# Sorting tokens by expert while attention still runs: scatter per batch in place of one-hot inverses

## The chip, the cores and the metric

The kernel runs on one core of a Trainium2 chip. The metric is the device time of one execution in microseconds (us); three runs of the kernel before are given by their median. A profile of one further execution shows its engines: PE (TensorE matmuls), PEld (TensorE weight loads), DVE (VectorE), ACT (ScalarE), POOL (GpSimd), SP (SyncE, which here only issues DMAs).

## The reference

Two stages, eight batches of 576 tokens. First block-causal attention, eight heads of 64; a token of block i (64 tokens) sees blocks 0 to i:

```python
scores = scale * np.matmul(q, k.transpose(0, 1, 3, 2))       # q, k, v: (8, 8, 576, 64) f32
scores = np.where(block_i >= block_j, scores, -1000000000.0)
attn = softmax(scores); x = np.matmul(attn, v)               # x: (8, 576, 512)
```

Then each token goes to one of eight experts, and a token whose local gate is at least 0.5 takes the expert of the token before it:

```python
for b in range(B):
    prev_e = -1
    for s in range(S):
        fresh_e = int(np.argmax(logits[b, s]))                # logits = x @ w_gate
        e = fresh_e if s == 0 or local_gate[b, s] < 0.5 else prev_e
        prev_e = e
        p = softmax(logits[b, s])
        h = np.maximum(x[b, s] @ w1[e], 0.0)                  # w1: (8, 512, 1024)
        out[b, s] = p[e] * (h @ w2[e])                        # w2: (8, 1024, 512)
```

## The kernel before

**Attention** runs 32 iterations, one for a batch and two of its heads; four iterations make a batch. An iteration is a pipeline over several pairs: PE computes the scores of the next pair (L492, in three groups of banks), DVE their row maxima (`maxima`, L508), ACT the exponentials and their sums `rs` (`exps`, L516); PE transposes the probabilities of this pair (L526), DVE and ACT copy them to `pt`, PE multiplies by V (`attend`, L553), DVE copies the result to `ot` (L558). `inverse` (L562 to L567) adds the two sums of the last block and writes the reciprocals to `rv` with six DVE operations. `finish`, one iteration later, has PE turn `ot` and form the gate logits in the same matmul (L578); DVE multiplies by `rv`, the logits into `tmp` (L582) and the values into `xt` (L585); Pool adds the logits up (L590, L591); SP writes `xt` to `x_rows` in DRAM (L593, L594). Sixteen loads of expert weights, 1 MB each, are issued on Pool (L383) behind the gate adds of chosen iterations, from iteration 2 on. Instructions that are "pinned" keep the order of the program on their engine. `rs`, `nm` and `tmp` have two buffers each.

**Routing** has two calls: `routing(0)` for batches 0 to 5, its steps spread by `MIDDLE` and `BEHIND` over iterations 24 to 31, and `routing(1)` for batches 6 and 7, spread over the FFN's first tiles. It finds each token's own expert (L163 to L182), sends that through DRAM (`a_dram`, `row`) to have tokens along the free axis, carries the expert on by a scan (L202), returns through DRAM (`e_dram`, `ecr`), and ranks tokens within experts by matmuls with a triangle of ones. Each token so has a slot. The inverse, which token stands in a slot, comes from one-hots of the slot (`hot`, L336, L339, L343), matmuls of them (L350) and sums (L354, L356); its results are `tok_g` (row to gather), `tok_s` (row to scatter) and `pslot` (the probability).

**FFN** runs over 43 tiles of 128 slots, 20 of the first part, 23 of the second. All weights lie in SBUF. Per tile Pool gathers rows of `x_rows` (L665), PE transposes them (L674), DVE copies `xb` (L677) and the tile's first weights `wt` (`fetch`, L691); PE multiplies (`up`, L700), ACT applies relu (L707), but DVE the second half of it for tiles from 18 on (L709); PE multiplies by the second weights (L714), ACT scales by `pslot` (L719), and Pool scatters the rows to the output (L720). Outside attention the order on an engine is chosen by a scheduler when the program is built.

Of the kernel before, what the change touches and what calls it, by code (L numbers as in the profile page):

```python
# [16 lines left out]
def kernel(  # L17
# [11 lines left out]
    nc = tc.nc  # L29
# [38 lines left out]
    lg_all = w_p.tile([P, B * NJ, E + 1], F32, tag="lg_all", name="lg_all")  # L68

    x_dram = nc.dram_tensor("x_rows", [BS, Dm], BF16).ap()  # L70
# [4 lines left out]


    NB0 = 6
    NC0 = NB0 * NJ
    NT0 = -(-(NB0 * S - E * (P - 1)) // P)
    PARTS = [(0, NC0, NT0), (NC0, NC_, NT - NT0)]  # L80
    NTM = max(NT0, NT - NT0)

    OUT = 8192.0
# [12 lines left out]
    K = Const()  # L96

    def route_constants():
        K.id_b = rt([P, P], BF16, "id_b")
        nc.gpsimd.tensor_copy(K.id_b, id_f)  # L100
        K.iota_e = rt([P, E], F32, "iota_e")
        nc.gpsimd.iota(K.iota_e, pattern=[[1, E]], base=0, channel_multiplier=0,
                       allow_small_or_imprecise_dtypes=True)
        K.desc_e = rt([P, E], F32, "desc_e")
        nc.gpsimd.tensor_scalar(K.desc_e, K.iota_e, -1.0, float(E), op0=ALU.mult, op1=ALU.add)
        K.thr = rt([P, NTM], BF16, "thr")
        nc.gpsimd.iota(K.thr, pattern=[[1, NTM]], base=0, channel_multiplier=0,
                       allow_small_or_imprecise_dtypes=True)
        K.iota_lo = rt([P, P], BF16, "iota_lo")
        nc.gpsimd.iota(K.iota_lo, pattern=[[1, P]], base=0, channel_multiplier=0,  # L110
                       allow_small_or_imprecise_dtypes=True)
        K.ones_b = rt([P, P], BF16, "ones_b")
        nc.gpsimd.memset(K.ones_b, 1.0)

        tri_f = rt([P, P], F32, "tri_f", tag="big")
        nc.gpsimd.memset(tri_f, 1.0)
        nc.gpsimd.affine_select(out=tri_f, in_=tri_f, compare_op=ALU.is_gt, fill=0.0,
                                base=0, pattern=[[1, P]], channel_multiplier=-1)
        K.tri_b = rt([P, P], BF16, "tri_b")
        nc.gpsimd.tensor_copy(K.tri_b, tri_f)  # L120
        K.ones_e = rt([P, NC0 * E], BF16, "ones_e")
        nc.gpsimd.memset(K.ones_e, 1.0)

        K.val = rt([P, NC_, 5], BF16, "val")
        tmp = rt([P, NC_], F32, "chunk_id", tag="eqm")
        nc.gpsimd.iota(tmp, pattern=[[S // 64, B], [2, NJ]], base=0, channel_multiplier=0,
                       allow_small_or_imprecise_dtypes=True)
        nc.gpsimd.tensor_copy(K.val[:, :, 0], tmp)
        tmp = rt([P, 1], F32, "part1", tag="mx")
        nc.gpsimd.iota(tmp, pattern=[[0, 1]], base=1, channel_multiplier=1,  # L130
                       allow_small_or_imprecise_dtypes=True)
        nc.gpsimd.tensor_copy(K.val[:, :, 1], tmp.to_broadcast([P, NC_]))
        K.oh = rt([P, E, NC_], BF16, "oh")
        K.slot = rt([P, NC_], F32, "slot")
        K.off = rt([P, E], F32, "off")
        K.sub = rt([P, E], F32, "sub")
        K.taken = rt([P, E], F32, "taken")
        K.cnt = rt([P, E], F32, "cnt")

    pslots = [rt([P, x[2]], F32, "pslot%d" % k) for k, x in enumerate(PARTS)]  # L140
    tok_gs = [rt([P, x[2]], I32, "tok_g%d" % k) for k, x in enumerate(PARTS)]
    tok_ss = [rt([P, x[2]], I32, "tok_s%d" % k) for k, x in enumerate(PARTS)]
    te_is = [rt([1, x[2]], I32, "te_i%d" % k) for k, x in enumerate(PARTS)]

    def routing(k, ew, last, psum, pin):

        c0, c1, nt = PARTS[k]
        n = c1 - c0
        b0, b1 = c0 // NJ, c1 // NJ
        a_dram = nc.dram_tensor("a_dram%d" % k, [2, b1 - b0, NJ * P], BF16).ap()  # L150
        e_dram = nc.dram_tensor("e_dram%d" % k, [b1 - b0, NJ * P], BF16).ap()
        dve = nc.vector
        rows = [P, n, E]

        def ts(out, in_, a, b, op0=ALU.mult, op1=ALU.add):
            pin(dve.tensor_scalar(out, in_, a, b, op0=op0, op1=op1))

        def each(ap):
            return ap[:, :, None].to_broadcast([P, E, n])

        lg = lg_all[:, c0:c1, :E]
        mx = rt([P, n], F32, "mx")
        pin(dve.reduce_max(mx, lg, axis=AX))  # L163
        mx3 = mx[:, :, None].to_broadcast(rows)

        eqm = rt(rows, F32, "eqm")
        pin(dve.tensor_tensor(eqm, lg, mx3, op=ALU.is_ge))
        pin(ew.tensor_mul(eqm, eqm, K.desc_e[:, None, :].to_broadcast(rows)))
        ep = rt(rows, F32, "ep")
        pin(ew.tensor_sub(ep, lg, mx3))  # L170
# [3 lines left out]
        best = rt([P, n], F32, "best")  # L174
        pin(dve.reduce_max(best, eqm, axis=AX))
        ak = rt([P, 2, n], F32, "ak")
        pin(dve.tensor_single_scalar(ak[:, 1, :], lg_all[:, c0:c1, E], 0.0, op=ALU.is_ge))
        pin(dve.memset(ak[0:1, 1, 0:n:NJ], 0.0))
        ts(best, best, -1.0, float(E))
        nkeep = rt([P, n], F32, "nkeep")  # L180
        ts(nkeep, ak[:, 1, :], -1.0, 1.0)
        pin(dve.tensor_mul(ak[:, 0, :], best, nkeep))  # L182
# [5 lines left out]
        pin(nc.tensor.transpose(ps[:2 * n, :P], ak.rearrange("p a c -> p (a c)"), id_f))  # L188
        akT = rt([2 * n, P], BF16, "akT")
        pin(nc.scalar.copy(akT, ps[:2 * n, :P]))  # L190
        nc.sync.dma_start(out=a_dram.rearrange("a b (t p) -> (a b t) p", p=P), in_=akT)
        row = rt([b1 - b0, 2, S], BF16, "row", tag="ring", bufs=2)
        nc.sync.dma_start(out=row, in_=a_dram[:, :, :S].rearrange("a b s -> b a s"))
        sm = rt([P, n], F32, "sm")
# [5 lines left out]
        erow = rt([b1 - b0, NJ * P], BF16, "erow", tag="ring", bufs=2)  # L200
        pin(dve.memset(erow[:, S:], 0.0))
        pin(dve.tensor_tensor_scan(erow[:, :S], row[:, 1, :], row[:, 0, :], 0.0,  # L202
                                   op0=ALU.mult, op1=ALU.add))
        nc.sync.dma_start(out=e_dram, in_=erow)
        ecr = rt([n, P], BF16, "ecr", tag="akT")
        nc.sync.dma_start(out=ecr, in_=e_dram.rearrange("b (t p) -> (b t) p", p=P))
        yield

        ps = psum()
        pin(nc.tensor.matmul(ps[:, :n], lhsT=ecr, rhs=K.id_b[:n, :n], start=True, stop=True))  # L210
        eix = rt([P, n], F32, "eix", tag="best")
        pin(dve.tensor_copy(eix, ps[:, :n]))

        oh = K.oh[:, :, c0:c1]
        pin(dve.tensor_tensor(oh, eix[:, None, :].to_broadcast([P, E, n]),
                              K.iota_e[:, :, None].to_broadcast([P, E, n]), op=ALU.is_equal))
        pin(dve.memset(K.oh[64:, :, c0 + NJ - 1:c1:NJ], 0.0))

        pin(ew.tensor_mul(ep, ep, oh.rearrange("p e c -> p c e")))
# [4 lines left out]
        for x, m in enumerate((K.tri_b, K.ones_b)):  # L224
            pin(nc.tensor.matmul(ps[:, x * n * E:(x + 1) * n * E].rearrange(
                "p (e c) -> p e c", e=E), lhsT=m, rhs=oh, start=True, stop=True))
        rc = rt([P, 2, E, n], F32, "rc", tag="big")
        rc2 = rc.rearrange("p x e c -> p (x e c)")
        pin(nc.scalar.copy(rc2, ps[:, :2 * n * E]))
        pg = rt([P, n], F32, "pg")  # L230
        pin(dve.reduce_sum(pg, ep, axis=AX))
        pin(dve.tensor_mul(pg, pg, sm))
        pin(dve.tensor_copy(K.val[:, c0:c1, 2], pg))
        for j in (3, 4):
            pin(dve.tensor_sub(pg, pg, K.val[:, c0:c1, j - 1]))
            pin(dve.tensor_copy(K.val[:, c0:c1, j], pg))
        yield

        inc = rt([P, E, n], F32, "inc", tag="eqm")
        pin(dve.tensor_tensor_scan(inc.rearrange("p e c -> p (e c)"), K.ones_e[:, :n * E],  # L240
                                   rc[:, 1].rearrange("p e c -> p (e c)"), 0.0,
                                   op0=ALU.mult, op1=ALU.add))

        pin(dve.tensor_sub(inc, inc, rc[:, 1]))
        pin(dve.tensor_add(rc[:, 0], rc[:, 0], inc))
        cnt = rt([P, E], F32, "cnt_n")
        pin(dve.tensor_add(cnt, inc[:, :, n - 1], rc[:, 1, :, n - 1]))
        pin(dve.tensor_sub(cnt, cnt, inc[:, :, 0]))
        yield

        ci = rt([P, 2, E], I32, "ci")
        til = rt([P, E], F32, "til")
        end = rt([P, E], F32, "end")
        exc = rt([P, E], F32, "exc")
        base = rt([P, E], F32, "base")

        def tiles(c):
# [525 lines left out]
```

## Time and profile before

| | |
|---|---|
| median of three runs | 627.66 us (626.38 to 628.62) |
| the profiled execution | 625.85 us, its span 623.8 us |
| TensorE's mean granted clock | 0.975 |
| busy share of the span | PE 90%, DVE 73%, ACT 53%, Pool 25% |
| first score matmul (L492) | starts at 13.86 us |
| last `inverse` of attention (L562) | starts at 411.5 us |
| first up matmul of the FFN (L700) | starts at 429.81 us |
| scaled output of tile 0, of tile 42 (L719) | 436.4 us, 610.5 us |
| weight loads (L383) | 16, a median of 10.2 us from issue to landing |

The profile's page has the busy share of each engine in 40 slices, groups of instructions by line with their time, count, mean and the idle time ahead of them with what ended it ("<-DVE nm" means that a write of DVE to nm came last). Windows give busy time by stretch; the timeline lists instructions in order of their start with their duration.

### The profile page before, as it was taken

How to read it: one execution, taken by the hardware profiler on the slowest of the kernel's cores; microseconds unless marked ns; L12 is line 12 of the kernel's file. 1: busy time of each engine (PE TensorE's matmuls, PEld its weight loads, DVE VectorE, ACT ScalarE, POOL GpSimd, SP SyncE). 2: the span in 40 equal slices, each digit the busy share in tenths (PEclk: the TensorE clock that was granted, in tenths of full speed). 3: DMA queues.
4: the chain of work that ended last, by engine and by line, in shares of the span. 5: the costliest groups of instructions: out<-in, count | busy, mean ns of one | idle time of the engine just before them, and what ended most of it. 6: DMA issues, size and time to landing. Idle time of an engine off the chain costs nothing. (4 is left out here: it accounts for less than half of the span.)

```text
span 623.8 us, 15804 instructions
## 1 busy us (share of the span) xinstructions
PE 563.6 (90%) x5586; PEld 396.2 (64%) x5586; DVE 452.7 (73%) x1403; ACT 329.4 (53%) x1057; POOL 155.3 (25%) x218
## 2 busy tenths in 40 slices
PE   2899999999999999999999998765989899999991
PEld 1567667677677677666766665554667677766660
DVE  1688888888888888888888788894588855555540
ACT  1676676666666676666666765601444343323320
POOL 3000010010000001001010010144565565666532
PEclk9999999999999999999999999986999999999996
DMA  8246596595958668695874746102232222222210
GB/s 165 55 96 115 116 158 117 120 177 102 170 123 158 103 131 163 114 182 109 153 136 96 136 90 113 23 10 61 78 104 77 99 89 78 94 91 90 82 56 0
DMA packets 154078, 65.99 MB, mean 106 GB/s; under 512 B 138010, under 2 KB 146226, under 8 KB 154002
## 3 DMA queue, kind: packets, MB, share of 16 engines
q0 software_dynamic: 18048, 31.86, 24.8%
q1 hardware_dynamic: 132466, 32.52, 24.2%
q10 hardware_dynamic: 3488, 0.61, 0.6%
q8 instruction: 46, 0.75, 0.5%
q14 instruction: 30, 0.25, 0.1%
HBM read 67.55 MB, written 16.02 MB: 134 GB/s over the span
## 5 line engine op out<-in xcount | busy, mean ns | idle before, releaser
L516 ACT ACTIVATE pb<-ps_s,nm 128x512 f32<-128x512 f32 (+4 forms) x320 | 158.3, 501 | 97.8 <-DVE nm L508 97.3
L508 DVE TENSOR_REDUCE nm<-ps_s 128x1 f32<-128x512 f32 (+4 forms) x320 | 134.5, 453 | 54.0 <-ACT pb L516 31.8
L526 PE MATMUL ps_p<-id_f,pb 128*128 128x128 f32 (+1 forms) x800 | 105.1, 282 | 11.4 <-ACT pb L516 8.0
L492 PE MATMUL ps_s<-kT,qT 64*64 64x512 f32 (+7 forms) x1280 | 100.7, 419 | 6.1 <-ACT qT L475 6.1
L526 PEld LDWEIGHTS ps_p<-id_f,pb 128*128 128x128 f32 (+1 forms) x800 | 86.3, 141 | 24.7 <-ACT pb L516 10.0
L590 POOL TENSOR_TENSOR tmp<-tmp 128x45 f32<-128x45 f32 x32 | 8.5, 264 | 356.9 <-DVE tmp L582 356.9
L700 PEld LDWEIGHTS <-wt 128*128 128x128 bf16 x1376 | 81.1, 98 | 21.1 <-issue 15.8
L553 PE MATMUL ps_o<-pt,vt 128*64 128x320 f32 (+4 forms) x896 | 93.6, 360 | 0.0
L700 PE MATMUL ps_h<-xb,wt 128*128 128x128 bf16 x1376 | 84.3, 220 | 9.3 <-DVE xb L677 9.1
L714 PE MATMUL ps_o<-w_bf,hT 128*128 x344 | 86.6, 379 | 0.4
L553 PEld LDWEIGHTS ps_o<-pt,vt 128*64 128x64 f32 x896 | 59.3, 137 | 35.8 <-DVE tmp L582 4.9
L707 ACT ACTIVATE hT<-ps_h 128x512 bf16<-128x512 f32 x61 | 36.4, 597 | 79.1 <-PE ps_h L700 79.1
L720 POOL DMA_INDIRECT out_dram<-o_sb,tok_s x43 | 54.5, 1268 | 63.8 <-DMA out_dram<-o_sb,tok_s 21.0
L492 PEld LDWEIGHTS ps_s<-kT,qT 64*64 64x64 f32 x1280 | 45.4, 134 | 38.2 <-issue 23.6
L691 DVE COPY wt<-w_bf 128x4096 bf16 x43 | 53.1, 1238 | 15.5 <-PE ps_h L700 13.0
L516 ACT ACTIVATION_READ_ACCUMULATOR pb<-ps_s,nm 128x1 f32 x320 | 64.3, 201 | 0.0
L665 POOL DMA_INDIRECT xg<-x_rows,tok_g x43 | 55.3, 1286 | 22.6 <-PE ps_x L674 9.3
L719 ACT ACTIVATE o_sb<-ps_o,pslot 128x512 f32<-128x512 f32 x43 | 29.5, 687 | 44.0 <-PE ps_o L714 38.3
L709 DVE TENSOR_SCALAR hT<-ps_h 128x512 bf16<-128x512 f32 x25 | 17.3, 691 | 48.1 <-PE ps_h L700 48.1
L578 PE MATMUL ps_n<-wg,ot 128*128 128x146 f32 x320 | 49.4, 303 | 0.0
L541 ACT COPY pt<-ps_p 64x128 f32<-64x128 f32 (+2 forms) x102 | 43.6, 441 | 10.5 <-PE ps_p L526 10.3
L714 PEld LDWEIGHTS <-hT 128*128 128x128 bf16 x344 | 31.2, 98 | 24.8 <-issue 1.1
(147 smaller groups left out, 568.7 us busy)
## 6 DMA issues: line engine op xcount, KB each, us to landing
w_bf<-in_moe_w_dram POOLq DMA_DIRECT2D x16, 1024.0 KB, 10.2
natq<-in_q_dram SPq DMA_DIRECT2D x64, 128.0 KB, 2.6
vt<-in_v_dram SPq DMA_DIRECT2D x64, 128.0 KB, 4.7
natk<-in_k_dram SPq DMA_DIRECT2D x60, 128.0 KB, 2.7
x_rows<-xt SPq DMA_DIRECT2D x32, 128.0 KB, 2.6
natq<-in_q_dram SPq DMA_DIRECT2D x32, 32.0 KB, 2.5
vt<-in_v_dram SPq DMA_DIRECT2D x32, 32.0 KB, 6.3
natk<-in_k_dram SPq DMA_DIRECT2D x30, 32.0 KB, 2.2
```

The lines of the kernel that those rows point to most:

```text
L492: pin(nc.tensor.matmul(ps[y][f * 64:(f + 1) * 64, c:c + n], lhsT=qT[r, i * 64:(i + 1) * 64], rhs=kT[r, a:a + n], start=True, stop=True))
L508: pin(nc.vector.reduce_max(nm[:, z:z + 1], ps[g][y][:, c:c + n], axis=AX, negate=True))
L516: pin(nc.scalar.activation(pb[i][:, a:a + n], ps[g][y][:, c:c + n], func=AF.Exp, bias=nm[:, i:i + 1], accum_out=rs[:, z:z + 1]))
L526: pin(nc.tensor.transpose(ps[:kk, (c + e) * P:(c + e + 1) * P], pb[i0 + 2 * e][:, j * P:j * P + kk], id128))
L541: pin(cp(dst, src))
L553: pin(nc.tensor.matmul(ps[h * D:(h + 1) * D, a - q0:qn], lhsT=vts[i % 3][:, j, h, :], rhs=pt[j][:, h, a - j * P:a - j * P + n], start=(j = ...
L578: pin(nc.tensor.matmul(ps[:, (t - t0) * (P + WG):(t - t0 + 1) * (P + WG)], lhsT=ot[:, t * P:(t + 1) * P], rhs=wg[:, hp], start=True, stop= ...
L665: nc.gpsimd.indirect_dma_start(out=xg[:], out_offset=None, in_=x_dram[:rows], in_offset=bass.IndirectOffsetOnAxis(ap=tok_gs[k][:, u:u + 1] ...
L691: nc.vector.tensor_copy(wt.rearrange("p k f -> p (k f)"), w1_bf[:, bass.ds(o, WE)])
L700: nc.tensor.matmul(ps_h[:, f, :], lhsT=wt[:, ko, fo * P:(fo + 1) * P], rhs=xb[:, ko * P:(ko + 1) * P], start=(ko == 0), stop=(ko == KO1 - 1))
L714: nc.tensor.matmul(ps_o, lhsT=hT[:, fo, :], rhs=w2_bf[:, bass.ds(woff + fo * Dm, Dm)], start=(fo == 0), stop=(fo == FO - 1))
L720: nc.gpsimd.indirect_dma_start(out=out_flat, out_offset=bass.IndirectOffsetOnAxis(ap=tok_ss[k][:, u:u + 1], axis=0), in_=o_sb[:], in_offse ...
```

## The change

The rows of x are no longer written to DRAM in token order and gathered through an inverse. `finish` writes them to a tile of the batch, `x_b`, whose rows carry two more words: the token's number and its probability. As soon as a batch is complete, `routing(b)` works on that batch alone, by the same steps, with a running count `K.free` of the next free row of each expert's region in `x_sorted`; then five indirect DMAs scatter its rows to those regions, each through a view of its own, so that no scatter waits for another. The steps are hooked to iterations, nine places for each batch. `table(k)` computes from the counts which rows a tile gathers and which expert it has; the one-hots, `tok_g`, `tok_s` and `pslot` are gone. Tiles now read the token's number and probability from the gathered rows.

With it come: `inverse` takes one reciprocal on DVE and six copies on Pool; two buffers of V in place of three, with its loads later; k of the second pair and the gate weights are loaded from SP, and an Exp of one column is put ahead of the first copies; the first part has 16 tiles instead of 20, so DVE takes relus from tile 14 on; the 16 gathers of the first part are issued early, three in iteration 30 and the others behind the last gate add; output scatters go through views of their own as well; the tiles from 36 on add a skip to the token's number (`tok_e`).

```diff
-    x_dram = nc.dram_tensor("x_rows", [BS, Dm], BF16).ap()
+    ROW = Dm // 2 + 2
+    xs = nc.dram_tensor("x_sorted", [E * BS, ROW], I32).ap()
+    xs_views = dram_disjoint_views(xs, B * NJ)
+    out_views = dram_disjoint_views(out_flat, NT)
     NB0 = 6
-    PARTS = [(0, NC0, NT0), (NC0, NC_, NT - NT0)]
+    PARTS = [NB0 * S // P - E - 3, 0]
+    PARTS[1] = NT - PARTS[0]
...
+    def routing(b, x, lg, psum, pin, ew):
+        ...
+        pin(dve.tensor_add(rk[:, :NJ], rk[:, :NJ], K.free[:, None, :].to_broadcast(full)))
+        pin(dve.tensor_mul(rk[:, :NJ], rk[:, :NJ], oh))
+        to = rt([P, NJ], F32, "to")
+        pin(dve.reduce_sum(to, rk[:, :NJ], axis=AX))
+        to_i = rt([P, NJ], I32, "to_i", bufs=2)
+        pin(dve.tensor_copy(to_i, to))
+        pin(dve.memset(to_i[64:, NJ - 1:], E * BS))
+        pin(dve.tensor_add(K.free, K.free, rk[:, NJ]))
+        yield
+        for c in range(NJ):
+            pin(pool.indirect_dma_start(
+                out=xs_views[b * NJ + c], out_offset=bass.IndirectOffsetOnAxis(ap=to_i[:, c:c + 1], axis=0),
+                in_=x[:, c, :], in_offset=None, bounds_check=E * BS - 1, oob_is_err=False))
+            if c == 2:
+                yield
+        yield
...
-        vts = [cst.tile([P, NJ, 2, D], F32, tag="v%d" % x, name="vt") for x in range(3)]
+        vts = [cst.tile([P, NJ, 2, D], F32, tag="v%d" % x, name="vt") for x in range(2)]
...
-                eng = nc.scalar if nm == "k" and i < 2 else nc.sync
+                eng = nc.scalar if nm == "k" and i == 0 else nc.sync
...
+        warm = rt([P, 1], F32, "warm")
+        nc.vector.memset(warm, 0.0)
+        pin(nc.scalar.activation(warm, warm, func=AF.Exp))
...
-            nc.scalar.dma_start(out=wg[r, :, c:c + E], in_=gsrc[h])
-            nc.scalar.dma_start(out=wg[r, :, c + E:c + E + 1], in_=lsrc[h])
+            nc.sync.dma_start(out=wg[r, :, c:c + E], in_=gsrc[h])
+            nc.sync.dma_start(out=wg[r, :, c + E:c + E + 1], in_=lsrc[h])
...
         def inverse(rs):
             pin(nc.vector.tensor_add(rs[:, NB - 1:NB], rs[:, NB - 1:NB], rs[:, NB:NB + 1]))
+            pin(nc.vector.reciprocal(rs[:, :NB], rs[:, :NB]))
             for f in range(2):
                 r = slice(f * 64, (f + 1) * 64)
-                pin(nc.vector.reciprocal(rv[:64, 0:1, f ^ swap[0]], rs[r, 0:1]))
-                pin(nc.vector.reciprocal(rv[:64, 1:, f ^ swap[2]], rs[r, 2:NB:2]))
-                pin(nc.vector.reciprocal(rv[64:, :NJ - 1, f ^ swap[1]], rs[r, 1:NB:2]))
+                pin(nc.gpsimd.tensor_copy(rv[:64, 0:1, f ^ swap[0]], rs[r, 0:1]))
+                pin(nc.gpsimd.tensor_copy(rv[:64, 1:, f ^ swap[2]], rs[r, 2:NB:2]))
+                pin(nc.gpsimd.tensor_copy(rv[64:, :NJ - 1, f ^ swap[1]], rs[r, 1:NB:2]))
...
+        def hook(i, half):
+            if half == 1 and i % HP == 0 and i > 0:
+                b = i // HP - 1
+                steps[b] = routing(b, *batches[b], psum, pin, pool)
+                plan(steps[b], [(i, 1), (i + 1, 0), (i + 1, 1), (i + 2, 0), (i + 3, 0),
+                                (i + 3, 1), (i + 4, 0), (i + 4, 1), (i + 5, 0)])
+                if b == NB0 - 1:
+                    plan(table(0, pin), [(i + 4, 1), (i + 5, 0), (i + 5, 1)])
+            for x in reversed(todo.get((i, half), ())):
+                next(x, None)
+            if (i, half) == (HP * NB0 + HP + 2, 1):
+                gather_early()
...
-            if n == 0 or t < NT0 - 2:
+            if n == 0 or t < N0 - 2:
                 nc.scalar.activation(dst, ps_h, func=AF.Relu)
...
+            tok = xgs[t][:, Dm // 2:Dm // 2 + 1]
+            if t >= NCT:
+                tok_e = f_p.tile([P, 1], I32, tag="tok_e", name="tok_e")
+                nc.vector.tensor_tensor(tok_e, tok, skip_i[:, t - NCT:t - NCT + 1], op=ALU.add)
+                tok = tok_e
...
-                out=out_flat,
-                out_offset=bass.IndirectOffsetOnAxis(ap=tok_ss[k][:, u:u + 1], axis=0),
+                out=out_views[t],
+                out_offset=bass.IndirectOffsetOnAxis(ap=tok, axis=0),
...
+        with tc.issue_after(gate_last.ins):
+            while len(xgs) < N0:
+                gather_next()
```

## The prediction

> **What bounds the kernel now.** I read the page's slices first: they show the stages, and each has its own limit.
>
> ```profile
> PE   2899999999999999999999998765989899999991
> DVE  1688888888888888888888788894588855555540
> ACT  1676676666666676666666765601444343323320
> POOL 3000010010000001001010010144565565666532
> ```
>
> One slice is 15.6 us. Attention fills slices 2 to 26 with PE at nine tenths and DVE at eight; a hole follows; then the FFN, where Pool and DVE are half busy. The hole, by stretches (columns: PE, PEld, DVE, ACT, POOL busy us, clock, DMA share, GB/s):
>
> ```profile
> 400.00:410.00 10.00, 6.80 (x63) 5.62 (x65) 8.78 (x33) 4.41 (x17) 4.50 (x13) 1.00 0.06 15
> 410.00:420.00 10.00, 5.32 (x44) 4.45 (x40) 9.13 (x39) 0.00 (x0) 4.20 (x10) 0.75 0.01 3
> 420.00:430.00 10.00, 1.47 (x12) 0.94 (x11) 4.93 (x18) 0.27 (x1) 5.72 (x6) 0.50 0.20 51
> ```
>
> DVE is full there with the one-hots of the inverse (L336 to L356), PE is not. Next one steady iteration, in the timeline of all engines, since the change rewrites its end:
>
> ```profile
> 174.74 0.27 POOL L591 TENSOR_TENSOR lg_all<-lg_all,tmp 128x45 f32<-128x45 f32 x1
> ...
> 177.34 3.19 PE L526 MATMUL ps_p<-id_f,pb 128*128 128x128 f32 x25
> 177.39 0.31 ACT L516 ACTIVATE pb<-ps_s,nm 128x64 f32<-128x64 f32 x1 [0.29 <-DVE nm L508]
> ...
> 178.00 0.15 DVE L562 TENSOR_TENSOR rs<-rs 128x1 f32<-128x1 f32 x1
> 178.07 0.15 DVE L565 RECIPROCAL rv<-rs 64x1 f32<-64x1 f32 x1
> ...
> 182.37 0.69 ACT L516 ACTIVATE pb<-ps_s,nm 128x512 f32<-128x512 f32 x1 [1.54 <-DVE nm L508]
> ```
>
> I count everything from L562: it starts exactly every 11.9 us from 35.2 to 320.8, one per iteration, and from there to 403.1 the six iterations with routing take 82.3 instead of 71.4. The next iteration's first exp stands 4.4 us after L562. Last, the FFN and its end, Pool's queue in time:
>
> ```profile
> L720 POOL DMA_INDIRECT out_dram<-o_sb,tok_s x43 | 54.5, 1268 | 63.8 <-DMA out_dram<-o_sb,tok_s 21.0
> ...
> 613.60 0.98 POOL L720 DMA_INDIRECT out_dram<-o_sb,tok_s  x1 [1.87 <-issue]
> 616.45 0.98 POOL L720 DMA_INDIRECT out_dram<-o_sb,tok_s  x1 [1.87 <-DMA out_dram<-o_sb,tok_s]
> ```
>
> The last scatters stand 2.85 us apart, each behind the landing of the one before (2.8 us in the list of DMA issues), and 616.45 is five us after the last o_sb (610.5 + 0.69).
>
> **The change, part by part.** All against the profiled execution: span 623.8, time 625.85, which is 1.8 below the median 627.66.
>
> *Start.* ACT's table load starts at 11.81 because ACT's queue first issues eight k loads and wg; it takes 1.28, qT's copy 0.71, and scores start at 13.86 after 6.09 us of PE idle for qT. kT is done at 8.30. With a table load ahead and wg on SP, scores can start when kT is there, 8.5: **-5.3**. SP's queue gets seven more issues of 0.5 us, behind the loads of pair 0; if they hold pair 1 or wg back, some of it is lost: -3 to -5.5.
>
> *Routing per batch, in attention.* Per batch some 20 DVE operations of 128x40 or less (the trace's 128x80 ones take 0.24, its 128x10 ones 0.17) and a scan (1.35, L202): about 4.7 us of DVE, 3.7 of it ahead of group-2 maxima. Price: in the trace the first two steps (0.40 + 0.41 behind L562, 1.3 ahead of the maxima) made the iteration from 320.8 take 13.11, that is +1.2 for 2.1 us of DVE. At that rate 2.7 per batch; but most pieces are below the 0.7 us for which exps end ahead of the transposes, and the inverse gives DVE back 0.75 in every iteration (six reciprocals of 0.15 to 0.17 become one, the copies go to Pool). I take 1.3 per batch, seven batches: **+9**; between 0 (all in DVE's idle sixth) and +19. In iterations without a step I count the 0.75 as nothing, since PE covers it; if it is not, 0.3 x 31 = 9 comes back. x_rows' 64 writes leave SP, 28 small DMAs come; SP is no bound.
>
> *Scatters and the new wait.* Behind step six four scatters of a batch are queued on Pool, and behind them the six copies rv<-rs. In the built order the fourth copy waits for the landing of all four scatters. rs has two buffers, so the next iteration's first exp on ACT waits for the copies: it stands 4.4 us after L562. Queued behind Pool's wait are the fifth scatter and the gate adds; behind ACT's exp, PE's transposes; DVE's multiplies (finish) wait for rv too. In iterations 12 and 16 the scatters start some 2.9 us ahead of L562, 1.31 apart (1.01 plus 0.30, as the gathers stand), so the last lands at -2.9 + 3.9 + 2.8 = +3.8, three to six copies of about 0.25 (L590 as the nearest row) end at 4.6 to 5.3: **+1** for both. In iterations 8, 20, 24 and 28 a weight load stands directly ahead of them on the same software queue. The trace has no indirect DMA behind a weight load, so two bounds. Landing as if alone: 1 us later than above, 0.4 past slack each, +1.6 in all. Landing behind the load's own bytes (10.2 us median; 8.5 and 11.7 the extremes): -2.9 + 10.2 + 0.7 = +8.0 (0.7 for their rows: the out scatters' median landing of 2.8 above their minimum of 2.1), copies +8.75, ACT 4.4 late, less the 0.7 of slack: 3.7 each, 2 to 5.2 by the extremes. I take the second, since q0 software_dynamic is one row of the page for loads and scatters alike and three scatters behind each other have no other ring: **+15**, range +1.6 to +21.
>
> The Trainium skill, DMA: Bandwidth & Descriptors (Queues, rings and completion order), says that on each DMA engine descriptors of one ring are consumed in ring order, and its section SWDGE vs HWDGE vs iDMA that only one software queue is allocated. The trace cannot show it here. By that rule the term is the +15, and the design's intent, scatters hidden behind attention, is broken in those four iterations; without it, +1.6.
>
> *table(0)* about 25 DVE operations of 0.17 to 0.8 in iterations 28 and 29, 5 us at the rate above: **+3** (0 to 5). *One-hot inverse gone:* 82.3 - 71.4: **-10.9**. Attention in sum 9 + 1 + 15 + 3 - 10.9 = +17.1.
>
> *The hole.* From the last L562 (411.5) to the first up matmul (429.81) 18.3 us: DVE's one-hots to 419.4, finish, then fetch, gather, transposes. After: the first tiles are gathered, and behind finish (1.5 us) DVE has two wt copies of 1.23 and xb 0.42; about 6 us: **-12.3** (-9 to -13).
>
> *FFN.* Relus of the second half go to DVE from tile 14 instead of 18 and DVE's order is wt, xb, relu throughout: the loop of the trace's tiles 28 to 42, where relu 0.69, wt 1.22, xb 0.42 and PE's 1.95 follow each other, 4.27. Tiles 14 to 27 took 50.0 for 13, 3.85: +5.5. tok_e for the spare tiles stands in DVE's queue near tile 22 and waits for a gather that, with 17 buffers, waits for the out of tile 19: +3. Batch 7's scan is followed directly by the one-hot that waits for its round trip through e_dram; between scan and matmul the trace shows 3.2 us, then partly covered by a wt copy of 1.23: +2. Routing of batches 6 and 7 with table(1), 12 us of small operations beside DVE's wt and xb, takes the place of the trace's (tiles 0 to 14 took 60.6 at 3.85 x 14 = 53.9): 0. In sum **+10.5**; from +2 (no loop, no spike) to +24 (below).
>
> *Tail.* Scatters go to views of their own, so the last is issued when its o_sb is there, 611.5 instead of 616.45: **-5**; 0 if Pool is late by itself.
>
> Sum: -5.3 + 17.1 - 12.3 + 10.5 - 5 = +5.0. 625.85 + 5.0 = 630.9, and 1.8 for the median: 632.7.
>
> **Rivals.** *No wait behind the weight loads* (the other side): the term is +1.6 instead of +15, the sum -8.4, 619.3. It decides at one place: if the four scatters of iterations 8, 20, 24 and 28 land by +4.4 after L562, ACT waits for nothing. For it speaks that a load and a scatter touch different memory and 16 engines share the work; against it the single queue. Between 610 (with 0.3 per iteration back) and 625.
>
> *Pool bounds the FFN:* 13 gathers, ten scatters, then per tile an out and a gather that waits for an earlier out's landing. Out and gather together 1.27 + 1.29 + 2 x 0.30 = 3.2 fit; but in 500 to 547 single outs averaged 1.45, and 1.02 + 0.30 + landing 2.8 in a row would be 4.2 plus 0.3 to 0.5: 4.6 a tile in tiles 4 to 42 instead of 4.2: +14 over my sum, 647. For it: Pool's 0.5 to 0.6 already; against: 8.1 us of its idle time there is for ACT, so it has room.
>
> *Small operations hide, and the reciprocals' 0.75 shows:* 0 instead of +9 and -3 from the steady iterations: 621 to 625 with the scatter waits. For it DVE's 84%; against it PE's full slices.
>
> **How the numbers follow.** Chances: forecast 0.45 (626 to 645), no wait 0.30, Pool 0.13, hidden operations 0.12. 0.3% of 627.7, about what a measurement can tell from no change, is 1.9 us. Faster (below 625.8): 0.27 of the no-wait case, 0.08 of the hidden, 0.03 of the forecast, together 0.38; same 0.06; slower 0.56. The range reaches into the no-wait and Pool cases: 612 to 650.
>
> **What would show it.** Right: ACT's first exp of iterations 9, 21, 25 and 29 idle for 3 to 5 us with Pool's rv copy as the releaser, and those intervals of the inverse (then L539) near 16 us; scores at 8.5; up matmul 6 us after the last inverse; tiles at 4.27 from 14 on; last out issue within 1.5 us of its o_sb. Wrong: those intervals at 12 to 13 (no wait), o_sb periods above 4.5 with Pool never idle (Pool), routing iterations at 11.9 (hidden). The forecast falls most simply if a scatter behind a weight load lands in 3 us.

## The result, and the profile after

The changed kernel takes 676.67 us (675.29 to 677.38, four runs) beside 627.02 (622.03 to 628.62): 1.080 of the time before, interval 1.074 to 1.087. The direction was right, the size was not: +50 where +5 stood. The profiled execution has a span of 675.3 at a granted clock of 0.951; before it was 623.8 at 0.975. All stages below compare these two.

The page's slices of after; one slice is 16.9 us:

```profile
PE   5999999879999999969969996877996762688986
DVE  3687788858878778758866885863742440345552
ACT  4666666456656656636636653513442221123322
POOL 2002122312322331422141342376884444442222
```

Two things are new. Attention has notches (ACT at 4, 3, 3, 3, PE at 7 or 6), and in the FFN PE falls to 6, 7, 6, 2, 6 just after Pool stood at 7, 6, 8, 8. This is one of the notches in the timeline of Pool, around iteration 20, whose weight load is L354:

```profile
282.46 0.80 POOL L354 DMA_DIRECT2D w_bf<-in_moe_w_dram  x1
283.56 1.07 POOL L265 DMA_INDIRECT x_sorted<-x_b,to_i  x1 [0.30 <-DVE nm L483]
...
287.55 0.98 POOL L265 DMA_INDIRECT x_sorted<-x_b,to_i  x1 [0.30 <-issue]
288.52 0.21 POOL L543 COPY rv<-rs 64x1 f32<-64x1 f32 x1
...
295.52 0.18 POOL L543 COPY rv<-rs 64x1 f32<-64x1 f32 x1 [6.45 <-DMA x_sorted<-x_b,to_i]
```

Three copies run at once, the fourth waits 6.45 us for the landing of four scatters that stand behind a load. On ACT, in its timeline, the next exp waits with it:

```profile
296.09 0.69 ACT L491 ACTIVATE pb<-ps_s,nm 128x512 f32<-128x512 f32 x1 [7.04 <-POOL rv L545]
```

The list of ACT's waits (total us, times, longest) has all six such exps together:

```profile
ACT pb L491 <- POOL rv L545: 31.1, 6, 7.4
```

The list of line L265, the scatters, says who waited for them (us, times) and how long they took to land:

```profile
  POOL rv L543: 28.0, 6
...
DMA to landing us min/median/max: 2.3/3.0/9.8
```

The hole is smaller. Windows of after, with the columns of the prediction's; last inverse (L539) at 441.52, first up matmul at 447.26:

```profile
430.00:440.00 10.00, 8.31 (x72) 6.30 (x70) 7.49 (x25) 4.29 (x17) 3.14 (x13) 1.00 0.00 1
440.00:450.00 10.00, 5.82 (x62) 5.27 (x59) 7.05 (x31) 1.03 (x3) 6.78 (x15) 0.79 0.08 20
450.00:460.00 10.00, 9.89 (x100) 7.68 (x101) 4.62 (x5) 4.50 (x8) 8.17 (x7) 0.87 0.31 88
```

In the FFN, DVE's timeline shows one long wait, and Pool's an even rhythm behind it:

```profile
555.72 0.42 DVE L662 COPY xb<-ps_x 128x512 bf16<-128x512 bf16 x1
578.33 0.16 DVE L705 CUSTOM_DVE_ANT_0 tok_e<-xg,skip_i 128x2 uint16<-128x2 uint16 x1 [22.19 <-DMA xg<-x_sorted,rows]
578.41 0.69 DVE L694 TENSOR_SCALAR hT<-ps_h 128x512 bf16<-128x512 f32 x1
```

```profile
565.78 1.02 POOL L146 DMA_INDIRECT xg<-x_sorted,rows  x1 [2.50 <-issue]
567.10 1.02 POOL L709 DMA_INDIRECT out_dram<-o_sb,xg  x1 [0.31 <-issue]
570.62 1.02 POOL L146 DMA_INDIRECT xg<-x_sorted,rows  x1 [2.50 <-issue]
```

A pair of gather and out takes 4.84 here: 1.02, a gap of 0.30, 1.02, and 2.50 until the out just issued has landed (this one at 569.89). Other pairs take up to 6.5; from the gather of tile 24 to that of tile 42 the mean is 5.2. The out at 567.10 is tile 18's, and reads the token numbers from its `xg`; the gather at 570.62 is tile 35's, and with 17 buffers overwrites that one. Pool's order lets each gather run ahead as far as the buffers allow, so each waits for the out directly ahead of it. The tail:

```profile
670.09 0.98 POOL L709 DMA_INDIRECT out_dram<-o_sb,tok_e  x1 [3.22 <-ACT o_sb L708]
671.82 0.98 POOL L709 DMA_INDIRECT out_dram<-o_sb,tok_e  x1 [0.74 <-ACT o_sb L708]
```

The outs wait for their o_sb now, not for each other. By stages, profiled against profiled:

| stage | predicted | measured |
|---|---|---|
| start, to the first inverse (35.2, now 31.0) | -5.3 | -4.2 |
| attention, first to last inverse (376.3, now 410.5) | +17.1 | +34.2 |
| hole, to the first up matmul (18.3, now 5.75) | -12.3 | -12.5 |
| FFN, to the last o_sb (180.7, now 223.6) | +10.5 | +42.9 |
| tail, to the end (13.3, now 4.5) | -5 | -8.8 |
| sum | +5.0 | +51.6 |

### The profile page after: what moved, and what is told of

It reads as the page before. It is cut to its first block, busy times and chain, and to the rows that moved or that the text cites. A ratio compares the mean times of both kernels' runs of the same rounds, so it can differ in the third digit from the quotient of the medians.

```text
span 675.3 us, 15911 instructions
## 1 busy us (share of the span) xinstructions
PE 575.7 (85%) x5519; PEld 407.0 (60%) x5548; DVE 428.3 (63%) x1276; ACT 323.3 (48%) x1054; POOL 229.2 (34%) x488
## 5 line engine op out<-in xcount | busy, mean ns | idle before, releaser
L699 PE MATMUL ps_o<-w_bf,hT 128*128 x315 | 84.0, 386 | 33.6 <-DVE hT L694 16.6
L685 PEld LDWEIGHTS <-wt 128*128 128x128 bf16 x1376 | 88.3, 104 | 29.1 <-issue 23.2
L685 PE MATMUL ps_h<-xb,wt 128*128 128x128 bf16 x1376 | 91.9, 230 | 15.4 <-DVE xb L662 11.1
L467 PE MATMUL ps_s<-kT,qT 64*64 64x512 f32 (+7 forms) x1280 | 103.8, 430 | 0.7 <-DVE kT L453 0.7
L558 PE MATMUL ps_n<-wg,ot 128*128 128x146 f32 x320 | 53.0, 317 | 19.4 <-ACT qT L450 19.0
L146 POOL DMA_INDIRECT xg<-x_sorted,rows x40 | 49.2, 1231 | 55.7 <-issue 23.8
L708 ACT ACTIVATE o_sb<-ps_o,xg 128x512 f32<-128x512 f32 x40 | 27.5, 688 | 74.4 <-DMA out_dram<-o_sb,xg 47.5
L558 PEld LDWEIGHTS ps_n<-wg,ot 128*128 128x128 f32 x320 | 45.4, 205 | 22.6 <-ACT qT L450 19.9
L694 DVE TENSOR_SCALAR hT<-ps_h 128x512 bf16<-128x512 f32 x29 | 20.1, 692 | 60.5 <-PE ps_h L685 60.4
L543 POOL COPY rv<-rs 64x1 f32<-64x1 f32 x64 | 11.8, 185 | 134.3 <-DVE rs L540 59.2
```

Of the source, the lines that this page charges most:

```text
L146: nc.gpsimd.indirect_dma_start(out=xg[:], out_offset=None, in_=xs, in_offset=bass.IndirectOffsetOnAxis(ap=rows[k][:, u:u + 1], axis=0), bo ...
L467: pin(nc.tensor.matmul(ps[y][f * 64:(f + 1) * 64, c:c + n], lhsT=qT[r, i * 64:(i + 1) * 64], rhs=kT[r, a:a + n], start=True, stop=True))
L558: pin(nc.tensor.matmul(ps[:, (t - t0) * (P + WG):(t - t0 + 1) * (P + WG)], lhsT=ot[:, t * P:(t + 1) * P], rhs=wg[:, hp], start=True, stop= ...
L685: nc.tensor.matmul(ps_h[:, f, :], lhsT=wt[:, ko, fo * P:(fo + 1) * P], rhs=xb[:, ko * P:(ko + 1) * P], start=(ko == 0), stop=(ko == KO1 - 1))
L699: nc.tensor.matmul(ps_o, lhsT=hT[:, fo, :], rhs=w2_bf[:, bass.ds(woff + fo * Dm, Dm)], start=(fo == 0), stop=(fo == FO - 1))
L708: nc.scalar.activation(o_sb, ps_o, func=AF.Copy, scale=xgs[t].bitcast(F32)[:, Dm // 2 + 1:])
```

## The experiments

Each is timed against the kernel before on the same chip; line numbers shift by a few with an edit.

**The reciprocals back on DVE.** Theory: Pool's copies carry the wait into attention, and it is worth 15. Rival: DVE's work is the cost.

```diff
-            pin(nc.vector.reciprocal(rs[:, :NB], rs[:, :NB]))
...
-                pin(nc.gpsimd.tensor_copy(rv[:64, 0:1, f ^ swap[0]], rs[r, 0:1]))
+                pin(nc.vector.reciprocal(rv[:64, 0:1, f ^ swap[0]], rs[r, 0:1]))
```

(and so for all six.) 

> Undoes one part: the six reciprocals are back on DVE, so no copy on Pool stands behind the scatters. Theory (Pool's copies wait for the landing of scatters that stand behind a weight load, and ACT's next exp waits for the copies): the four intervals of 18.1 to 19.8 us between inverses fall to 12.5 to 13.5, iterations without routing go from 11.65 back to 11.9, in sum -23 + 31 x 0.25 = -15, about 661 us. Rival (the scatters' traffic or the weight load itself slows the iteration): these intervals stay above 17 and the time goes up by 8, to 684.

668.86, 1.069 (1.067 to 1.071): a gain of 7.8, half of what was expected. The four intervals fall from between 18.1 and 19.8 to between 13.9 and 15.2, so the copies did carry the wait. But the scatters are as late as ever, and another operation now waits for them, DVE's write of the next batch's `x_b` in finish (L265's list of this kernel):

```profile
  DVE x_b L564: 6.0, 3
...
DMA to landing us min/median/max: 2.3/5.0/9.8
```

The late landing is the cause; who waits for it is interchangeable.

**The weight loads in other iterations.** The load is moved out of the iterations whose scatters stand behind it.

```diff
-                while done < min(2 * E, 2 * E * i // (NPR - 3)):
+                while done < min(2 * E, 2 * E * i // (NPR - 3)) and (i % HP or i < 2 * HP):
```

> Copies stay on Pool; weight loads are no longer issued in iterations 8, 12, 16, 20, 24 and 28, where they stood directly ahead of scatters, but one iteration later. Theory (one software queue serves in order): scatters land in 3 us instead of up to 9.8, the four long intervals fall to 13.3 as in iterations 12 and 16, -23, about 653 us. Rival (the copies' wait is long whatever stands ahead of the scatters): the intervals stay above 16, time above 668.

661.54, 1.059 (1.057 to 1.061). The scatter intervals become 14.1, 13.3, 13.3, 14.2, 13.3, and Pool's copies wait 7.4 in all where they waited 28.0 (the same list):

```profile
  POOL rv L543: 7.4, 6
...
DMA to landing us min/median/max: 2.3/3.1/5.2
```

The gain is 15, not 23, since the two loads pushed to the end of attention make the last intervals 14.8, 16.6 and 9.3, some 6 to 7 us longer.

**A copy of the same size beside the scatters, on another queue.** Is it the order of the queue, or the bytes in flight? The loads stay apart, and SP copies 1 MB to DRAM where the load stood.

```diff
+                if i % HP == 0 and i >= 2 * HP:
+                    with tc.issue_after(last.ins):
+                        nc.sync.dma_start(out=scratch[i // HP], in_=...)
```

> As the run with the loads apart, and SP copies 1 MB of weights from SBUF to DRAM on its own queue in each iteration where scatters are issued (the copy's result is not used). Theory 1 (the scatters waited in the software queue behind the load, not for the engines' bytes): with the same megabyte on another queue scatters still land in 3 to 4 us and the intervals behind them stay at 13 to 14.2. Theory 2 (a megabyte on the 16 engines delays whatever stands beside it): landings of 6 us and more, intervals above 16.

A single execution took 664.5. Over all scatters L265's landings stay near where they were without the copy:

```profile
DMA to landing us min/median/max: 2.7/3.2/5.5
```

But the copies, issued from 108.4 to 368.9, took only 4.4 to 6.0 us, where a load takes 8.5 to 11.7, and three of the six (iterations 8, 24 and 28) had landed 9 us or more ahead of the scatters. A copy was still in flight, for its last 2 to 3.5 us, when the scatters of iterations 12, 16 and 20 began. Their first four landed in 4.0 to 5.4, 3.2 to 3.8 and 4.8 to 5.9 us, beside 2.9 to 3.7, 2.8 to 3.8 and 3.1 to 5.2 without the copy, and the intervals behind them are 14.2, 13.3 and 15.8 beside 13.3, 13.3 and 14.2. So a copy on another queue goes with up to some 2 us more, less than the 4 to 8 that a scatter loses behind a load. Theory 1 is favoured but not shown by this run, since the copies were shorter than the loads and half of them passed early. The order in the trace of after speaks for it too: in all four iterations the load lands first (135.4, 292.7, 348.8, 406.9) and the first scatter, an eighth of its bytes and issued 1.1 to 1.3 us behind it, 0.5 to 1.7 us later.

**tok_e behind the last xb copy.** Theory 1: DVE's wait of 22.19 is the FFN's loss. Theory 2: it only shows how far Pool is behind.

```diff
-            nc.vector.tensor_copy(xb, ps_x)
+            xb_last[0] = nc.vector.tensor_copy(xb, ps_x)
...
-                nc.vector.tensor_tensor(tok_e, tok, skip_i[:, t - NCT:t - NCT + 1], op=ALU.add)
+                with tc.issue_after(xb_last[0].ins):
+                    nc.vector.tensor_tensor(tok_e, tok, skip_i[:, t - NCT:t - NCT + 1], op=ALU.add)
```

> Only the place of tok_e in DVE's queue changes: behind the xb copy of the tile before. Theory 1 (DVE stood 22.2 us in front of tok_e, which waited for the gather of tile 36): the 24.6 us step at tile 23 falls to about 5, and the time by 12 to 20, to 657 to 665 us. Theory 2 (Pool's alternation of gather and out at 4.86 us a tile is the bound and DVE's wait only hides it): the step goes, but tiles to the 30th stay at 4.86 and the time falls by less than 6, above 670.

671.59, 1.075 (1.073 to 1.078). The step of 24.6 us between two xb copies becomes 7.8, and tiles 24 to 34 take 4.3 to 6.5 each in its place. Pool is no faster: from the gather of tile 24 to that of tile 42 it takes 99.1 us where it took 93.9, in pairs as this one, whose gather starts 0.7 after the landing of the out ahead of it (569.89):

```profile
570.62 1.02 POOL L146 DMA_INDIRECT xg<-x_sorted,rows  x1 [3.45 <-issue]
571.95 1.01 POOL L712 DMA_INDIRECT out_dram<-o_sb,xg  x1 [0.30 <-issue]
```

Theory 2 holds: one wait of DVE turned into many, and Pool's pairs are the bound.

**Gathers behind the out of four tiles before their own.** The same instructions, another order on Pool.

```diff
-            nc.gpsimd.indirect_dma_start(
+            outs[t] = nc.gpsimd.indirect_dma_start(
...
+            if t0 in outs:
+                with tc.issue_after(outs[t0].ins):
+                    xgs.append(gather(t, xg))
...
-                gather_next()
+                gather_next(t - 1)
```

> Only Pool's order changes: a gather of the second part is issued behind the out scatter of four tiles before it, instead of as early as its buffer allows (17 tiles ahead). Theory (early gathers stand ahead of outs, so o_sb's four buffers fill, and each waits for the landing of the out just ahead of it: 1.02 + 0.30 + 3.5 = 4.86 us a tile): the 11.2 us step at tile 15 and the 4.86 us tiles go, tiles run at 4.27, and tok_e waits less: -28 to -35, 642 to 649 us. Rival (Pool needs 4.86 us for a pair in any order): no more than 5 us are gained.

651.64, 1.043 (1.041 to 1.045): 25 us back from an order alone. Pool's timeline now has the out waiting for its o_sb and the gather behind it for nothing, 4.26 a pair:

```profile
545.15 1.11 POOL L709 DMA_INDIRECT out_dram<-o_sb,xg  x1 [1.82 <-ACT o_sb L708]
546.56 1.04 POOL L146 DMA_INDIRECT xg<-x_sorted,rows  x1 [0.30 <-issue]
549.41 1.11 POOL L709 DMA_INDIRECT out_dram<-o_sb,xg  x1 [1.81 <-ACT o_sb L708]
```

Tiles 35 to 41 take 5.1 to 6.7, since tok_e, still early on DVE, waits 2.7 to 4.5 for gathers that are late now. So the two edits belong together.

**Both FFN orders.** 

> The changed kernel with gathers behind outs and tok_e behind xb, its weight loads as they were. If both causes of the FFN add, the 5 to 6.7 us tiles from the 35th on of the run with late gathers alone (651.6) go to 4.3: -11, about 641 us, with the four long intervals of attention still at 17 to 20. If late gathers and tok_e share their gain: 650.

642.93, 1.028 (1.022 to 1.035); nearly every tile from 15 on at 4.27. **And the loads apart with them.** 

> As the run before, with the loads apart as in the run with 661.5 us (and not spread otherwise). If the 15 to 17 us intervals behind scatters in the run of three orders come from where the loads stood there: 13 to 14.2 here and about 627 us. If they come from the other two edits or from the chip's state on that day: 15 us and more again, 640 us or above.

624.11, 0.9965 (0.994 to 0.999), 18.8 less on the same chip. Three orders of the same instructions take away all of the loss and a little more. **The same with the loads spread a little further**, `2 * E * i // (NPR - 5)` in place of `NPR - 3`: 

> The changed kernel with three changes of order and no other: weight loads spread so that none is issued in the iterations of the scatters and all by iteration 27; gathers of the second part behind the out of four tiles before; tok_e behind the xb copy. If the three causes add up (23 us of waits behind loads, 25 us of Pool's order, 11 us of tok_e behind late gathers in tiles 35 to 41), 676.7 - 59 = 618 us. If they cover each other, above 630.

659.56, 1.048 (1.044 to 1.051). That missed by 40, with intervals of 14.7 to 17.4 in the scatter iterations and a granted clock of 0.968. **ACT takes both relus as well** (`if n < 2:`): 

> As the run before, and ACT takes both relus of every tile instead of leaving the second to DVE from tile 14 on. Theory (the 4.27 us a tile are DVE's loop of relu 0.69, wt 1.22, xb 0.42 and the 1.95 us of PE between): tiles go to 3.7 us as tiles 7 to 14 show, 28 x 0.5 = -14, about 604 us. Rival (Pool's pair of DMAs or PE sets 4.27): less than 3 us gained.

663.38, 1.051 (1.048 to 1.055): no gain. DVE's timeline shows what took the relu's place:

```profile
602.28 1.23 DVE L678 COPY wt<-w_bf 128x4096 bf16 x1 [2.93 <-PE ps_h L687]
```

The weight copy waits for PE's ps_h 2.93, where in the run before it followed a relu of 0.69 that had waited 2.2 for the same. The wait is longer by the relu that is gone; why is open. The same two kernels with the loads apart and the loads spread were then run beside each other on another chip. 

> The same kernel as the run of three orders with 659.6 us, whose intervals behind scatters were 15 to 17 us although no load stood ahead of them. If the schedule of its loads makes them (two loads in iteration 17, one in iteration 7 and 23): again 15 to 17 us and about 655 us. If it was the chip on that day: 13 to 14 us at all of them, no long last intervals, and 618 to 622 us.

623.08, 0.998 (0.995 to 1.001), with a clock of 0.990, and 

> The same kernel as the run of three orders with the loads apart (624.1 us), beside the run above on one chip. If schedules decide: 624 us, 30 us less than the run above. If days decide: within 8 us of the run above, and slower than it by the late loads' 6 us.

622.12, 0.994 (0.992 to 0.997). The 659.56 and 663.38 stand beside a kernel before that took 630.23, slower than the 625 to 627 elsewhere; the program of 659.56 took 623.08 on the other chip, so its number says nothing of the schedule. What slowed it there is open. It was not the wait behind loads: Pool's copies waited 6.7 us in all for scatters, and 7.1 in the repeat.

**No scan.** 

> The changed kernel without the scan of each batch (tokens that should take the expert of the token before them take none of it, so experts and tiles are filled otherwise; only the intervals of attention are read). Theory (what DVE does ahead of group-2 maxima is paid in full): the interval with the scan, 13.1 us, falls to 11.7 to 11.8, since 1.30 of its 1.48 us go. Rival (my price of 0.58 us for each us of DVE work): it falls to 12.3.

A single execution took 672.9 (before 625.87). The intervals with the scan go from 13.1 or 13.2 to between 11.8 and 12.0, as the theory says and the rival does not. But the next ones go from 11.64 to 12.1: of the 1.1 to 1.4 gained, nearly 0.5 is given back. Over the two iterations a scan of 1.30 costs 0.65 to 0.9, which is the rival's rate.

**The change's other parts, put into the kernel before.** The start, one reciprocal and Pool's copies, and views for the output scatters, with the old routing:

```diff
+            pin(nc.vector.reciprocal(rs[:, :NB], rs[:, :NB]))
...
-                out=out_flat,
+                out=out_views[t],
```

> The kernel before with the three parts of the change that its trace shows as gains: the early table load with k of the second pair and wg on SP (-5.3), one reciprocal on DVE with six copies on Pool (11.65 instead of 11.9 us in iterations without routing, -7), output scatters in views of their own (-5). The sum, -17, gives 609 us. If the copies cost in routing iterations or the last outs are late by Pool itself, above 615.

616.42, 0.978 (0.976 to 0.981), -13.8: scores at 8.5 and intervals of 11.7 in place of 11.9 bring the last inverse from 411.5 to 399.5; the FFN gives some back, its later tiles at 4.5. **ACT takes both relus there too:** 

> As the run before, and ACT takes both relus of every tile. By DVE's loop: tiles 18 to 42 took 4.1 us on average and go to 3.75, -8, about 601 us. Rival (PE is full at 3.9 to 4.1 us a tile): no gain.

612.37, 0.971 (0.968 to 0.975), later tiles at 4.2: 4 more, half of what was expected. Both ran beside the 659.56 and the same slower kernel before (630.23), and were not repeated elsewhere; beside the 625 to 627 of the other runs they would be 9 to 11 and 13 to 15 faster. The 612.37 lies below every time of either kernel. Its tail, on Pool:

```profile
601.02 0.98 POOL L726 DMA_INDIRECT out_dram<-o_sb,tok_s  x1 [3.21 <-ACT o_sb L725]
602.75 0.99 POOL L726 DMA_INDIRECT out_dram<-o_sb,tok_s  x1 [0.75 <-ACT o_sb L725]
```

## Why the prediction was right and wrong

**Attention: the mechanism was right, two terms were mis-sized.** The forecast's wait is there: ACT's exps behind the weight loads, with Pool's rv as the releaser, four intervals of 18.1, 19.3, 19.8 and 19.6 where "near 16" stood. The exp came 9.5, 9.8, 10.2 and 8.4 us after its inverse, against the 4.4 + 4.4 that the working gives: the landing was estimated well, some 0.7 short. But the interval lost more than the exp was late. Measured against 13.33, the scatter interval without a load, the four lose 4.7, 5.9, 6.4 and 6.3, together 23.3 instead of 15: the later exps account for some 3 of the extra 8. Behind each wait TensorE ran slower, and the windows on either side of the second show it (clock is the third column from the end):

```profile
289.00:296.00 7.00, 3.17 (x30) 1.54 (x22) 3.41 (x9) 0.06 (x1) 0.51 (x4) 0.98 0.94 204
296.00:303.00 7.00, 5.80 (x40) 4.65 (x42) 3.32 (x12) 4.21 (x15) 1.92 (x6) 0.54 0.18 44
```

More than half of PE's time idle in the first, half the clock in the second; before, the same window has 1.00. The four spells at half clock begin at 138.7, 295.7, 353.7 and 411.7 and last 3.4, 6.8, 6.8 and 3.4 us. In the 3.4 us ahead of them TensorE did nothing three times and 0.65 us of work the fourth time. The Trainium skill, TensorE: Matmul & The Clock Gate (Part 1, on the HAM clock gate), says that the clock falls to half after an idle window of some 3.4 us and is full again after a busy one; these spells agree. How much of the extra they are was not separated from the rest.

The small operations were priced at 1.3 per batch, +9. They cost about 25, more than the +19 named as the most: the intervals with the first steps take 12.4, those with the scan 13.1, the last steps' 13.0 to 13.4, beside 11.65 without any. The trace of before had shown 1.2 for 2.1 us of DVE, the rate of +19, and I went below it for pieces "below the 0.7 us for which exps end ahead of the transposes"; that was the step that failed here. The run without the scan shows the one large piece near that rate, and the small pieces did not hide: steps of 1.1 to 1.8 us of DVE cost 0.8 to 1.7 an iteration. The scatters cost 0.9 in each of six iterations, not 0.5 in two. table(0), at +3, lies in the fourth of those intervals and cost less: in the runs that have no load ahead of its scatters that one takes 14.2 and 14.8, or 0.9 to 1.5 above 13.33. Against that, an iteration without routing gained 0.25, which I had at nothing (7.5 over the 30 iterations, since the prices above are measured from 11.65), and the one-hots' -10.9 came as worked out, with 1.2 more in the last interval. 25.0 + 5.4 + 23.3 - 7.5 - 10.9 - 1.2 is +34.1 of the 34.2.

**The FFN: a step failed.** The loop at 4.27 is right, for tiles 27 to 38 here and, with the orders mended, from 15 on; that DVE's relu is a needed link of it is not shown, as the run with both relus on ACT gained nothing. What I had at +3, "tok_e for the spare tiles stands in DVE's queue near tile 22 and waits for a gather", was 22.19 of idle DVE, because the gather itself stood in a Pool queue that took 4.8 us or more a pair from the gather of tile 24 on. That is the rival *Pool bounds the FFN*, which I gave 0.13 and 4.6 a tile: its mechanism was there, its arguments against ("8.1 us of its idle time there is for ACT, so it has room") judged Pool by its busy share, while its order had a landing in every pair. Measured by the starts of xb copies against before, the loss is 5.3 at tile 15, 15.5 at 22, 35.4 at 23 and 41.8 by 29. The order's part is shown: 25 by the gathers alone, 34 by gathers and tok_e. In the stage itself, 223.6 becomes 199.9 and then 185.9, which is +5.2 over before, near the +7.5 that stood beside the +3.

The first step, 11.2 us from one xb copy to the next at tile 15, falls where ACT waits, as its group on the page has it:

```profile
L708 ACT ACTIVATE o_sb<-ps_o,xg 128x512 f32<-128x512 f32 x40 | 27.5, 688 | 74.4 <-DMA out_dram<-o_sb,xg 47.5
```

47.5 us of waiting for outs that had not landed. The longest, 7.13, ends at 511.19: Pool had issued eight gathers and five scatters ahead of those outs, and the four o_sb buffers were full.

**The rest.** Hole -12.5 for -12.3, start -4.2 for -5.3 (-3.8 to -5.6 in the other runs; scores start at 8.51 as forecast), tail -8.8 for -5: the last issue follows its o_sb by 1.0 as worked out; beyond that the span ends 3.5 us after the issue where it ended 7.3 after it before. The kernel before with views for its outs still has 7.3, so the views do not explain it, and no run does.

**The other rivals.** *No wait behind the weight loads* is false: landings of 7.1 to 10.9 us behind a load, 2.3 to 4.0 in the iterations without. *Small operations hide* is false in its first half and right in its second (the 0.25 per iteration).

## What to carry to other kernels

An engine at half load can still be the bound when its instructions wait for landings of those ahead: look at a queue's order and the period of its pairs, not at its busy share. Before moving small DMAs into a stage, find the large ones on the same queue and keep them out of the iterations with the small ones; here that and two orders in the FFN were worth 53 us, the whole loss. And test the parts of a bundled change alone: three small ones without the new routing gave 9 to 14 us, while the whole, with its orders repaired, gave 2 to 4.

## What the runs showed of the hardware

Four scatters issued 1.3 us apart behind a 1 MB load on the software queue landed 0.3 to 0.4 apart right behind it in iteration 8 (the load at 135.4, they at 135.9, 136.2, 136.6 and 137.0), 8.0 to 10.9 us after their issue, and 7.1 to 10.9 over all four such iterations; in the iterations without a load they take 2.3 to 4.0. The Trainium skill, DMA: Bandwidth & Descriptors (Queues, rings and completion order), says that on each DMA engine descriptors are consumed in ring order, though a later one may finish its write first; these times agree with the order. Scatters that began beside a copy of the same size on SP's queue took 3.2 to 5.9. And behind idle spells of TensorE of 3.5 to 5.4 us its clock stood at a half for 3.4 or 6.8 us.
